# Retention and a multiplicative feed-forward on one core: loads put ahead of stores, scalings cut loose from the transposes, products moved to VectorE

## The chip, the core and the metric

The program runs on one of the eight cores of a Trainium2 chip. The metric is the device time of one execution in microseconds: 1075.24 us, the median of three runs (1071.42 to 1076.22). In the rows below, PE is TensorE's matmul, PEld its weight load, DVE VectorE, ACT ScalarE, POOL GpSimd and SP the engine whose queue issues nearly all DMAs.

## What is computed

A retention block (attention without a softmax, with a decay), and a feed-forward whose two branches are multiplied:

```
scores = q @ k.T / sqrt(64)                    # 8 batches x 8 heads, 576 positions, 64 wide
ret    = (scores * gamma_h ** (i - j), 0 for j > i) @ v
x      = ret, heads side by side               # 4608 tokens x 512
a, b   = x @ w1, x @ w2                        # 4608 x 1024 each
out    = ((a * b) @ w3) @ w_out                # 4608 x 512
```

The weights are given as 64-bit floats, the rest as 32-bit floats.

## The kernel before

**Attention.** Batches are taken in four pairs (i). A sequence of 576 is cut into five chunks of 64, 128, 128, 128 and 128 positions (c); g = 5 i + c counts the chunks. For each g, `load` brings k, q and v of the pair from memory (two buffers each). `front` scales q and v by the decay on GpSimd and transposes k and q on TensorE (`tp`), ScalarE copying the results. `state` multiplies k and v into a running state (`st`), which ScalarE copies to `sb`. `score` multiplies q and k, and VectorE masks the result (`pm`). `pv` adds the state's and the masked scores' share of the output (`xps`), which ScalarE copies to `xT`.

**Feed-forward.** The tokens of a pair are cut into three blocks of 2 x 192. `up(i, n, fp)` computes a quarter of a and b for one block by Strassen's scheme with seven products of half size, each of eight matmuls of 192 columns: the weight sums S1 to S4 are made once per quarter (`strassen_weights`), the token sums T once per block (`strassen_tokens`, on GpSimd). The seven products are put together by sums on VectorE (`plus`), and a times b goes to `ab`: one of the four slices on VectorE, three on GpSimd. w3 and w_out are multiplied with each other once (`w3_tr`, `w3_mm`), and `down` multiplies `ab` with the result, 128 tokens at a time, and stores it.

**Conversion.** The weights arrive as 40 blocks of 128 x 512 64-bit numbers in `raw` tiles and are made into 32-bit ones in five VectorE steps and two Relus on ScalarE each: three steps (`begin_block`: exponent e, mantissa m, low word added) and two (`end_block`: sign, product), with one block begun ahead of the one that is ended. The steps are a generator, and `convert(n)` draws n of them wherever it is called; this decides where they stand on VectorE's queue. The first 16 blocks are w1 and w2, four for each quarter, then 8 of w_out and 16 of w3.

**Order.** The order of every engine is that of the code: nothing is rearranged, and an engine that waits holds all that is behind it. The program has three stretches. In the first, the five chunks of pair 0 are worked off with the conversion and the first three `up`; then come the remaining nine `up` of pair 0 with w3 and w_out. In the second, `down` of pair 0 fills the chunks of pair 1. After that the `up` and `down` of each pair are spread by `work` over the chunks of the next. The lines that the change and the prediction's steps touch are `front`, `load_block`, `begin_block`, `up`, `down` and the loops at the end.

Of the kernel before, what the change touches and what calls it, by code (L numbers as in the profile page):

```python
# [32 lines left out]
def kernel(  # L33
# [72 lines left out]
    dq = ffn.tile([P, 3, 2, TB], F32, tag="c", name="dq").rearrange("p a b s -> p (a b s)")[:H, :S]  # L106
    nc.scalar.dma_start(dq, decay_q)
    for c in range(NC):
        for b in range(2):
# [21 lines left out]

    def strassen_weights(fp):
        def tt(out, in0, in1, op):
            nc.gpsimd.tensor_tensor(out=A(fp, out), in0=A(fp, in0), in1=A(fp, in1), op=op)  # L134

        tt("S1", "A21", "A22", ALU.add)
        tt("S2", "S1", "A11", ALU.subtract)
        tt("S3", "A11", "A21", ALU.subtract)
        tt("S4", "A12", "S2", ALU.subtract)
# [3 lines left out]
    def load(g, names):  # L143
# [3 lines left out]
        for nm in names:  # L147
# [2 lines left out]
                t[:sz], src[nm][2 * i:2 * i + 2, :, starts[c]:starts[c] + sz, :].rearrange("b h p d -> p (b h) d"))  # L150
            live[nm, g] = t

    def front(g):
        c = g % NC
        sz = sizes[c]
        kn, qn, vn = live["k", g], live["q", g], live["v", g]
        for t, gam in ((qn, gq), (vn, gk)):
            nc.gpsimd.tensor_tensor(  # L158
                out=t[:sz], in0=t[:sz],
                in1=gam[:sz, c].rearrange("p b h -> p (b h)").unsqueeze(2).to_broadcast([sz, 2 * H, D]),  # L160
                op=ALU.mult)
# [91 lines left out]
    def load_block():  # L253
        n = loaded[0]
        if n == len(blocks):
            return
        key, w = blocks[n]
        t = raw.tile([P, CV, 2], I32, tag="raw", name="raw", bufs=4)
        if key[0] == "w12":
            _, fp, _, r = key  # L260
            src = w[2 * r * P:2 * (r + 1) * P, fp * QC:(fp + 1) * QC, :]
            for half in range(2):
                for_rows = src.rearrange("(c a d) n t -> a d c n t", a=2, d=D)[half ^ r]
                nc.sync.dma_start(t[heads[half]].rearrange("p (c n) t -> p c n t", c=2), for_rows)
# [18 lines left out]
    def begin_block():  # L283
        n = begun[0]
        t = live["raw", n]
        lo, hi = t[:, :, 0], t[:, :, 1]
        e = raw.tile([P, CV], I32, tag="exp", name="e")
        m = raw.tile([P, CV], I32, tag="man", name="m")
        vec = nc.vector


        vec.tensor_scalar(out=e, in0=hi, scalar1=1, scalar2=21,  # L292
                          op0=ALU.logical_shift_left, op1=ALU.logical_shift_right)
        relu = mybir.ActivationFunctionType.Relu
        nc.scalar.activation(e, e, relu, bias=lim[:, 0:1], scale=-1.0)  # L295
        nc.scalar.activation(e, e, relu, bias=lim[:, 1:2], scale=-2.0 ** 23)
        yield

        vec.tensor_scalar(out=m, in0=hi, scalar1=0x000FFFFF, scalar2=0x00100000,  # L299
                          op0=ALU.bitwise_and, op1=ALU.bitwise_or)  # L300
        yield
        vec.scalar_tensor_tensor(m.bitcast(F32), in0=lo.bitcast(U32), scalar=2.0 ** -32, in1=m,  # L302
                                 op0=ALU.mult, op1=ALU.add)
        live["em", n] = e, m
        begun[0] += 1
        yield
# [83 lines left out]
    def up(i, n, fp, conv=0):  # L390
        m = every.index((i, n))
        convert_up_to(4 * (fp + 1))
        if ("B", i, n) not in live:
            strassen_tokens(i, n)
        if fp == 0:
            live["ab", i, n] = (ab3 if m == 2 else ffn).tile([P, 2 * KF, TB], F32, tag="ab", name="ab")
        ab = live["ab", i, n]
        f = 4 * fp
# [12 lines left out]
        def plus(name, ps, sb, out=None):  # L411
            out = ffn.tile([P, 2, TB], F32, tag=name, name=name, bufs=1) if out is None else out
            nc.vector.tensor_add(out, ps, sb)  # L413
            convert(conv)
            return out


        c = ffn.tile([P, 3, 2, TB], F32, tag="c", name="c")
        p1 = product(None, "A11", "B11")
        p1s = ffn.tile([P, 2, TB], F32, tag="p1s", name="p1s", bufs=1)  # L420
        nc.scalar.copy(p1s, p1)
        u2 = plus("u2", product(None, "S2", "T2"), p1s)
        u3 = plus("u3", product(None, "S3", "T3"), u2)
        p5 = product(None, "S1", "T1")
        plus("c22", p5, u3, out=c[:, 2])
        plus("c21", product(None, "A22", "-T4"), u3, out=c[:, 1])
        product(p1, "A12", "B21")
        c11 = ffn.tile([P, TB], F32, tag="c11", name="c11")
        nc.scalar.copy(c11, p1[:, 0, :])  # L429
        nc.vector.tensor_mul(ab[:, f, :], p1[:, 1, :], c11)  # L430
        product(p5, "S4", "B22")
        plus("c12", p5, u2, out=c[:, 0])
# [5 lines left out]
    def down(i, n, t):  # L438
# [9 lines left out]
        while a < (t + 1) * P:  # L448
            b = a // TB
            e = min((b + 1) * TB, (t + 1) * P)  # L450
            r = (2 * i + b) * S + n * TB + a - b * TB
            nc.sync.dma_start(out[r:r + e - a, :], ot[a - t * P:e - t * P])
            a = e


    load(0, "kqv")
    load(1, "kqv")
    for _ in range(4):
        load_block()
    front(0)  # L460
    state(0)
    score(0)
    for g in range(NC):
        if g + 2 < NC:
            load(g + 2, "kvq")
        if g + 1 < NC:
            front(g + 1)
        pv(g)
# [27 lines left out]
    w3_part.close()  # L496


    pools["ot"] = ctx.enter_context(tc.tile_pool(name="ot", bufs=2, reuse_waits="tile"))
# [4 lines left out]
    open_attention(ctx)  # L504
    todo = [(down, 0, n, t) for n in range(2) for t in range(NT)]

    def add_pair(i):
# [12 lines left out]
            fn, *args = todo.pop(0)  # L520
            fn(*args)

    load(NC, "kqv")
    load(NC + 1, "kqv")
    work(1)
    front(NC)
    state(NC)
    score(NC)
    for g in range(NC, G):
        c = g % NC  # L530
        n = -(-len(todo) // (NC - c))
        if g + 2 < G:
            load(g + 2, "kv")
        if g + 1 < G:
            front(g + 1)
        if g + 2 < G:
            load(g + 2, "q")
        work((n + 1) // 2)
        pv(g)
        if g + 1 < G:  # L540
            state(g + 1)
            score(g + 1)
        work(n // 2)
        if c == NC - 1:
            add_pair(g // NC)
# [44 lines left out]
```

## Time and profile before

| | |
|---|---|
| median of three runs | 1075.24 us |
| profiled execution | 1074.96 us |
| its span, first to last instruction | 1073.2 us |
| mean granted clock of TensorE | 0.936 |
| TensorE matmul busy | 942.3 us (88%) |
| VectorE busy | 322.8 us (30%) |
| GpSimd busy | 216.5 us (20%) |
| ScalarE busy | 196.2 us (18%) |
| DMA | 59.69 MB, 56 GB/s over the span |

The shares are means over stretches with different limits: the first 320 us hold the conversion of the weights and more than half of VectorE's work, and TensorE's clock is below its upper level in many slices there. Reading starts with the stretches apart, and in each with who waits for whom.

### The profile page before, as it was taken

What the parts mean: (1) busy time and instruction counts of PE and PEld (TensorE: products, weight loads), DVE (VectorE), ACT (ScalarE), POOL (GpSimd) and SP (SyncE); (2) the same over time, 40 slices, a digit from 0 to 9 for tenths busy, and PEclk for the clock granted to TensorE, in tenths of its full rate; (3) what the DMA queues carried; (4) which work ended last, traced back from release to release, by engine and by line L of the source; (5) the groups of instructions that cost most, each with busy time, mean ns of one, the idle gap of its engine ahead of it and who ended that gap; (6) DMA issues with size and microseconds to landing.
All of it is one profiled execution on the core that took longest, in us unless ns stands there. A gap on an engine that the chain in (4) does not pass through costs nothing.

```text
span 1073.2 us, 14017 instructions
## 1 busy us (share of the span) xinstructions
PE 942.3 (88%) x6085; PEld 743.6 (69%) x6085; DVE 322.8 (30%) x581; ACT 196.2 (18%) x373; POOL 216.5 (20%) x159
## 2 busy tenths in 40 slices
PE   4456568899999787779898998999989999999998
PEld 4356468787644554479668688598687795959694
DVE  2445778865500100023112222122122230303120
ACT  2313323332311221111111111111111201000000
POOL 3142332311000311132204103113032020302110
PEclk9767879889999888889999998999999999999999
DMA  9744323322003732233030230212402000000000
GB/s 170 145 89 99 79 79 99 99 97 79 20 1 66 151 70 59 49 70 60 0 89 1 50 65 5 60 30 45 104 1 50 21 1 30 1 20 11 20 10 30
DMA packets 126382, 59.69 MB, mean 56 GB/s; under 512 B 114536, under 2 KB 114536, under 8 KB 126320
## 3 DMA queue, kind: packets, MB, share of 16 engines
q1 hardware_dynamic: 124992, 58.73, 24.0%
q8 instruction: 48, 0.79, 0.3%
q10 hardware_dynamic: 1328, 0.06, 0.1%
q14 instruction: 14, 0.11, 0.0%
HBM read 49.34 MB, written 9.44 MB: 55 GB/s over the span
## 4 chain that ended last, share of the span: by engine, by line
PE 75%; DVE 8%; DMA 6%; POOL 4%; issue 3%; ACT 2%; SPq 1%; ACTq 0%; POOLq 0%; DVEq 0%
PE up L407 36%; PE po L442 23%; PE ps L365 5%; DMA ld_q<-in_q_dram 4%; PE xps L233 3%; PE tp L169 3%; PE sc L184 2%; POOL ld_q L158 2%; DVE m L302 2%; DVE e L313 1%; PE xps L226 1%; POOL wS L134 1%; SPq L149 1%; PE st L205 1%; DVE m L299 1%
## 5 line engine op out<-in xcount | busy, mean ns | idle before, releaser
L442 PE MATMUL po<-w3o,ab 128*128 128x512 f32 x576 | 259.4, 609 | 0.0
L407 PE MATMUL up<-xT,wA 128*128 128x192 f32 x1152 | 225.6, 341 | 18.7 <-DVE wA L322 15.1
L407 PEld LDWEIGHTS up<-xT,wA 128*128 128x128 f32 x1152 | 201.9, 200 | 24.5 <-DVE wA L322 16.3
L442 PEld LDWEIGHTS po<-w3o,ab 128*128 128x128 f32 x576 | 111.6, 196 | 134.6 <-issue 133.0
L436 POOL TENSOR_TENSOR ab<-c 128x576 f32<-128x576 f32 x48 | 69.9, 1455 | 549.6 <-DVE c L413 540.7
L407 PE MATMUL up<-T,wS 128*128 128x192 f32 x768 | 149.0, 339 | 23.6 <-POOL wS L134 14.7
L407 PEld LDWEIGHTS up<-T,wS 128*128 128x128 f32 x768 | 135.1, 200 | 25.3 <-POOL wS L134 15.6
L187 DVE TENSOR_TENSOR pm<-sc,mask 128x512 f32<-128x512 f32 (+1 forms) x80 | 45.6, 629 | 280.9 <-PE sc L184 280.8
L413 DVE TENSOR_TENSOR u<-up,p1s 128x384 f32<-128x384 f32 x48 | 26.8, 557 | 263.2 <-PE up L407 176.5
L413 DVE TENSOR_TENSOR c<-up,u 128x384 f32<-128x384 f32 x144 | 80.0, 556 | 77.1 <-PE up L407 76.4
L158 POOL TENSOR_TENSOR ld_q<-ld_q,gq 128x1024 f32<-128x1024 f32 (+1 forms) x20 | 38.4, 1918 | 214.1 <-DMA ld_q<-in_q_dram 214.1
L169 PE MATMUL tp<-ident,ld_q 128*128 128x128 f32 (+1 forms) x160 | 26.4, 324 | 59.1 <-POOL ld_q L158 59.1
L407 PE MATMUL up<-xT,wS 128*128 128x192 f32 x384 | 72.7, 334 | 5.1 <-DVE c L413 5.1
L407 PE MATMUL up<-T,wA 128*128 128x192 f32 x384 | 70.4, 326 | 1.0 <-ACT ot L445 1.0
L407 PEld LDWEIGHTS up<-xT,wS 128*128 128x128 f32 x384 | 65.1, 194 | 6.5 <-DVE c L413 6.5
L445 ACT COPY ot<-po 128x512 f32<-128x512 f32 x36 | 21.1, 586 | 260.8 <-PE po L442 230.7
L407 PEld LDWEIGHTS up<-T,wA 128*128 128x128 f32 x384 | 63.7, 190 | 1.3 <-ACT ot L445 1.3
L169 PEld LDWEIGHTS tp<-ident,ld_q 128*128 128x128 f32 (+1 forms) x160 | 21.5, 175 | 62.2 <-POOL ld_q L158 62.2
L365 PE MATMUL ps<-wo,w3T 128*128 128x512 f32 x128 | 56.7, 595 | 1.2 <-ACT w3T L359 1.2
L429 ACT COPY c<-up 128x192 f32<-128x192 f32 x48 | 15.1, 315 | 228.4 <-PE up L407 228.4
L295 ACT ACTIVATE e<-e,lim 128x512 int32<-128x512 int32 x40 | 28.9, 722 | 134.6 <-DVE e L292 134.6
L365 PEld LDWEIGHTS ps<-wo,w3T 128*128 128x128 f32 x128 | 23.9, 190 | 28.9 <-issue 26.8
(51 smaller groups left out, 711.8 us busy)
## 6 DMA issues: line engine op xcount, KB each, us to landing
ld_k<-in_k_dram SPq DMA_DIRECT2D x16, 512.0 KB, 5.9
ld_q<-in_q_dram SPq DMA_DIRECT2D x16, 512.0 KB, 7.1
ld_v<-in_v_dram SPq DMA_DIRECT2D x16, 512.0 KB, 4.6
raw<-in_moe_w_dram SPq DMA_DIRECT2D x32, 256.0 KB, 4.6
raw<-in_moe_w_dram SPq DMA_DIRECT2D x16, 512.0 KB, 3.4
out_dram<-ot SPq DMA_DIRECT2D x24, 256.0 KB, 2.4
raw<-in_moe_w_out_dram SPq DMA_DIRECT2D x8, 512.0 KB, 3.5
out_dram<-ot SPq DMA_DIRECT2D x24, 128.0 KB, 2.4
```

Source lines behind the costliest of these rows:

```text
L158: nc.gpsimd.tensor_tensor(out=t[:sz], in0=t[:sz], in1=gam[:sz, c].rearrange("p b h -> p (b h)").unsqueeze(2).to_broadcast([sz, 2 * H, D]), ...
L169: nc.tensor.transpose(tp[:, p, :sz], src[:sz, h:h + 2, :].rearrange("p a d -> p (a d)"), ident[:sz, :sz])
L184: nc.tensor.matmul(sc[j][:sz, p, :sz], kT[hs, b, p, :sz], qT[hs, b, p, :sz], start=True, stop=True)
L187: nc.vector.tensor_mul(pm[:sz, b, j, :, :sz], sc[j][:sz, :, :sz], mask[:sz, :sz].unsqueeze(1).to_broadcast([sz, NP, sz]))
L233: nc.tensor.matmul(banks[r][heads[half], b, n, :sz], vs[:sz, b * H + 2 * p + j, :], pm[:sz, b, j, p, :sz], start=(c == 0 and m == 0), stop ...
L295: nc.scalar.activation(e, e, relu, bias=lim[:, 0:1], scale=-1.0)
L302: vec.scalar_tensor_tensor(m.bitcast(F32), in0=lo.bitcast(U32), scalar=2.0 ** -32, in1=m, op0=ALU.mult, op1=ALU.add)
L365: nc.tensor.matmul(ps, live["w3T", ft][:, g, :], live["wo"][:, g, :], start=(g == 0), stop=(g == KF - 1))
L407: nc.tensor.matmul(ps[:, w, :], a[:, w, r, :], b[:, r, :], start=(new and w == r == 0), stop=(w == r == 1), skip_group_check=True)
L413: nc.vector.tensor_add(out, ps, sb)
L436: nc.gpsimd.tensor_tensor(out=ab[:, f + 1:f + 4, :], in0=c[:, :, 0, :], in1=c[:, :, 1, :], op=ALU.mult)
L442: nc.tensor.matmul(po, ab[:, f, t * P:(t + 1) * P], live["w3o"][:, f, :], start=(f == 0), stop=(f == KF - 1))
```

## The change

The loads of q and k stand ahead of v's and of the stores, with v's behind `pv`; the scalings of q and v are calls of their own (`scale`), placed apart from the transposes; the first loads of pair 1 stand ahead of three `down` blocks' stores, which are kept in a list (`later`), with a third `ot` tile. The weight sums and the product a times b go from GpSimd to VectorE, the product over all four slices at once, and the sums of `up` work in place in one tile `c` of four slices instead of in tiles of their own. The copy of a's first slice to SBUF takes both slices. One more `raw` tile is loaded ahead; the Relus are issued behind the third step; and the calls of `convert` are spread anew: one step at each sum and one at each product instead of two at each sum, and the steps ahead of `score` instead of behind it.

```diff
     def strassen_weights(fp):
         def tt(out, in0, in1, op):
-            nc.gpsimd.tensor_tensor(out=A(fp, out), in0=A(fp, in0), in1=A(fp, in1), op=op)
+            nc.vector.tensor_tensor(out=A(fp, out), in0=A(fp, in0), in1=A(fp, in1), op=op)
...
+    def scale(g, nm):
+        c = g % NC
+        sz = sizes[c]
+        t, gam = live[nm, g], {"q": gq, "v": gk}[nm]
+        nc.gpsimd.tensor_tensor(
+            out=t[:sz], in0=t[:sz],
+            in1=gam[:sz, c].rearrange("p b h -> p (b h)").unsqueeze(2).to_broadcast([sz, 2 * H, D]),
+            op=ALU.mult)
...
-        t = raw.tile([P, CV, 2], I32, tag="raw", name="raw", bufs=4)
+        t = raw.tile([P, CV, 2], I32, tag="raw", name="raw", bufs=5)
...
         vec.scalar_tensor_tensor(m.bitcast(F32), in0=lo.bitcast(U32), scalar=2.0 ** -32, in1=m,
                                  op0=ALU.mult, op1=ALU.add)
+        relu = mybir.ActivationFunctionType.Relu
+        nc.scalar.activation(e, e, relu, bias=lim[:, 0:1], scale=-1.0)
+        nc.scalar.activation(e, e, relu, bias=lim[:, 1:2], scale=-2.0 ** 23)
...
-        def plus(name, ps, sb, out=None):
-            out = ffn.tile([P, 2, TB], F32, tag=name, name=name, bufs=1) if out is None else out
-            nc.vector.tensor_add(out, ps, sb)
+        def plus(ps, to, sb):
+            nc.vector.tensor_add(c[:, to], ps, c[:, sb])
             convert(conv)
...
+        c = ffn.tile([P, 4, 2, TB], F32, tag="c", name="c")
         p1 = product(None, "A11", "B11")
-        p1s = ffn.tile([P, 2, TB], F32, tag="p1s", name="p1s", bufs=1)
-        nc.scalar.copy(p1s, p1)
-        u2 = plus("u2", product(None, "S2", "T2"), p1s)
...
+        nc.scalar.copy(c[:, 0], p1)
+        plus(product(None, "S2", "T2"), 1, 0)
+        plus(product(None, "S3", "T3"), 2, 1)
         p5 = product(None, "S1", "T1")
+        plus(p5, 3, 2)
+        plus(product(None, "A22", "-T4"), 2, 2)
         product(p1, "A12", "B21")
-        c11 = ffn.tile([P, TB], F32, tag="c11", name="c11")
-        nc.scalar.copy(c11, p1[:, 0, :])
-        nc.vector.tensor_mul(ab[:, f, :], p1[:, 1, :], c11)
+        nc.scalar.copy(c[:, 0], p1)
         product(p5, "S4", "B22")
+        plus(p5, 1, 1)
...
-        nc.gpsimd.tensor_tensor(out=ab[:, f + 1:f + 4, :], in0=c[:, :, 0, :], in1=c[:, :, 1, :], op=ALU.mult)
+        nc.vector.tensor_mul(ab[:, 4 * fp:4 * fp + 4, :], c[:, :, 0, :], c[:, :, 1, :])
+        convert(conv)
...
     for g in range(NC):
-        if g + 2 < NC:
-            load(g + 2, "kvq")
-        if g + 1 < NC:
-            front(g + 1)
+        if g + 1 < NC:
+            if g + 2 < NC:
+                load(g + 2, "kq")
+            scale(g + 1, "q")
+            front(g + 1)
+            scale(g + 1, "v")
         pv(g)
+        if g + 2 < NC:
+            load(g + 2, "v")
+        if g == 1:
+            strassen_tokens(0, 0)
         if g + 1 < NC:
             state(g + 1)
+            if g == 1:
+                convert_up_to(KD)
+            else:
+                convert(10)
             score(g + 1)
-        convert(10)
         if 0 < g < NC - 1:
             up(0, 0, g - 1, conv=1)
-            convert(6)
...
         if todo:
-            up(*todo.pop(0), conv=2)
+            up(*todo.pop(0), conv=1)
...
-        convert(10 if not todo else 2)
+        convert(10 if not todo else 3)
...
     for t in range(NT):
-        down(0, 2, t)
+        down(0, 2, t, later=True)
...
+    for g in (NC, NC + 1):
+        load(g, "kqv")
+    store()
...
     for g in range(NC, G):
         if g + 2 < G:
-            load(g + 2, "kv")
+            load(g + 2, "kq")
         if g + 1 < G:
+            scale(g + 1, "v")
             front(g + 1)
-        if g + 2 < G:
-            load(g + 2, "q")
         work((n + 1) // 2)
         pv(g)
+        if g + 2 < G:
+            load(g + 2, "v")
         if g + 1 < G:
             state(g + 1)
             score(g + 1)
+        if g + 2 < G:
+            scale(g + 2, "q")
         work(n // 2)
```

On SP's queue, in the second stretch, these rows stand behind one another in the kernel before: the stores of `down` (`out_dram`) and the loads of two chunks.

```order
L452 DMA out_dram<-ot 128x512
L149 DMA ld_k<-in_k_dram 128x16x64
L149 DMA ld_v<-in_v_dram 128x16x64
L149 DMA ld_q<-in_q_dram 128x16x64
L452 DMA out_dram<-ot 64x512 x2
L149 DMA ld_k<-in_k_dram 128x16x64
L149 DMA ld_v<-in_v_dram 128x16x64
L149 DMA ld_q<-in_q_dram 128x16x64
```

And these stand there now:

```order
L149 DMA ld_k<-in_k_dram 128x16x64
L149 DMA ld_q<-in_q_dram 128x16x64
L460 DMA out_dram<-ot 64x512 x2
L149 DMA ld_v<-in_v_dram 128x16x64
L149 DMA ld_k<-in_k_dram 128x16x64
L149 DMA ld_q<-in_q_dram 128x16x64
```

The load of q no longer stands behind that of the same chunk's v, but behind the v of the chunk before it; the store of the `down` in between stands ahead of v.

At the start of the second stretch the loads of pair 1 follow the stores of the first `down` blocks on SP in the kernel before:

```order
L267 DMA raw<-in_moe_w_dram 128x1024 x16
L452 DMA out_dram<-ot 128x512
L452 DMA out_dram<-ot 64x512 x2
L452 DMA out_dram<-ot 128x512
L149 DMA ld_k<-in_k_dram 64x16x64
L149 DMA ld_q<-in_q_dram 64x16x64
```

Now they follow the last load of weights:

```order
L271 DMA raw<-in_moe_w_dram 128x1024 x16
L149 DMA ld_k<-in_k_dram 64x16x64
L149 DMA ld_q<-in_q_dram 64x16x64
L149 DMA ld_v<-in_v_dram 64x16x64
L149 DMA ld_k<-in_k_dram 128x16x64
L149 DMA ld_q<-in_q_dram 128x16x64
L149 DMA ld_v<-in_v_dram 128x16x64
L460 DMA out_dram<-ot 128x512
```

All six loads moved past the stores.

On VectorE, between the first and the second `up` block, these rows stood in the kernel before (c is the sum of `up`, e, m and wA the conversion, pm the masked scores):

```order
L413 TENSOR_TENSOR c<-up,u_516 128x384
L322 SCALAR_TENSOR_TENSOR wA<-m,e 128x2x256
L292 TENSOR_SCALAR e<-raw 128x512
L299 TENSOR_SCALAR m<-raw 128x512
L302 SCALAR_TENSOR_TENSOR m<-raw,m 128x512
L313 SCALAR_TENSOR_TENSOR e<-raw,e 128x512
L322 SCALAR_TENSOR_TENSOR wA<-m,e 128x2x256
L292 TENSOR_SCALAR e<-raw 128x512
L187 TENSOR_TENSOR pm<-sc,mask 128x512 x4
```

Now the masks and the weight sums (wS) stand like this, with the product (ab) eleven conversion steps ahead of the masks, of which the last three are shown:

```order
L317 SCALAR_TENSOR_TENSOR e<-raw,e 128x512
L326 SCALAR_TENSOR_TENSOR wA<-m,e 128x2x256
L296 TENSOR_SCALAR e<-raw 128x512
L191 TENSOR_TENSOR pm<-sc,mask 128x512 x4
L300 TENSOR_SCALAR m<-raw 128x512
L303 SCALAR_TENSOR_TENSOR m<-raw,m 128x512
L317 SCALAR_TENSOR_TENSOR e<-raw,e 128x512
L326 SCALAR_TENSOR_TENSOR wA<-m,e 128x2x256
L134 TENSOR_TENSOR wS<-wA 128x512
L134 TENSOR_TENSOR wS<-wS,wA 128x512
```

Eleven steps now stand between the block and the masks, where six stood behind the block's last sum and its step; four are left behind the masks, where ten stood, and the weight sums follow them on the same queue.

On ScalarE, ahead of the first `up` block, the Relus (L295 and L296 before) stood like this:

```order
L295 ACTIVATE e<-e,lim 128x512
L296 ACTIVATE e<-e,lim 128x512
L172 COPY kT<-tp 128x512 x2
L172 COPY qT<-tp 128x512 x2
L237 COPY xT<-xps 128x2x2x128 x2
L209 COPY sb<-st 128x512
```

The same copies now, with the Relus of blocks 2 and 3 (L306 and L307) behind them:

```order
L176 COPY kT<-tp 128x512 x2
L176 COPY qT<-tp 128x512 x2
L241 COPY xT<-xps 128x2x2x128 x2
L213 COPY sb<-st 128x512
L306 ACTIVATE e<-e,lim 128x512
L307 ACTIVATE e<-e,lim 128x512
L306 ACTIVATE e<-e,lim 128x512
L307 ACTIVATE e<-e,lim 128x512
```

Before, three blocks' Relus stood ahead of those copies, now two.

## Rows read from the trace of the kernel before

**Rows 1.** Busy by stage: span, PE, PEld, DVE, ACT, POOL (counts), clock, DMA share, GB/s.

```profile
0.00:319.50 319.50, 239.59 (x1525) 198.06 (x1526) 175.58 (x305) 94.65 (x162) 74.59 (x57) 0.87 0.36 89
319.50:468.50 149.00, 115.88 (x898) 72.22 (x897) 12.84 (x24) 26.95 (x52) 26.54 (x15) 0.87 0.42 84
468.50:1073.20 604.70, 586.80 (x3664) 473.31 (x3663) 134.37 (x252) 74.62 (x159) 115.37 (x88) 0.99 0.14 31
```

**Rows 2.** TensorE's waits from 319.5 to 468.5: us in total, times, longest.

```profile
PE tp L169 <- POOL ld_q L158: 32.0, 6, 6.9
```

**Rows 3.** TensorE's waits from 468.5 to the end.

```profile
PE tp L169 <- POOL ld_q L158: 12.7, 4, 3.3
```

**Rows 4.** Chain of waits, second stage: start us, us, what.

```profile
366.32 6.84 DMA ld_q<-in_q_dram
...
387.02 1.92 PE xps L233 x32
389.00 0.37 SPq L149
```

**Rows 5.** TensorE's timeline, first stage: start, us, engine, line, operation.

```profile
64.27 2.93 PE L407 MATMUL up<-T,wS 128*128 128x192 f32 x8 [8.91 <-POOL T L381]
...
75.11 1.04 PE L169 MATMUL tp<-ident,ld_k 128*128 128x128 f32 x8
...
99.06 2.93 PE L407 MATMUL up<-T,wS 128*128 128x192 f32 x8 [4.86 <-POOL wS L134]
...
132.53 2.93 PE L407 MATMUL up<-T,wS 128*128 128x192 f32 x8 [4.92 <-POOL wS L134]
...
156.66 2.93 PE L407 MATMUL up<-T,wS 128*128 128x192 f32 x8 [4.92 <-POOL wS L134]
...
217.52 1.92 PE L357 MATMUL tp<-ident,w 128*128 128x128 f32 x8
```

**Rows 6.** VectorE's timeline, first stage.

```profile
77.93 2.12 DVE L299 TENSOR_SCALAR m<-raw 128x512 int32<-128x512 int32 x1
...
88.35 2.48 DVE L187 TENSOR_TENSOR pm<-sc,mask 128x512 f32<-128x512 f32 x4 [4.20 <-PE sc L184]
...
93.61 0.42 DVE L299 TENSOR_SCALAR m<-raw 128x512 int32<-128x512 int32 x1
...
95.39 0.69 DVE L322 SCALAR_TENSOR_TENSOR wA<-m,e 128x512 f32<-128x512 f32 x1
```

**Rows 7.** GpSimd's timeline, the same place.

```profile
77.69 2.08 POOL L158 TENSOR_TENSOR ld_q<-ld_q,gq 128x1024 f32<-128x1024 f32 x1
```

**Rows 8.** Chain of waits, last stage, work that follows on itself.

```profile
599.50 0.93 PE st L205 x32
...
616.35 1.75 PE tp L169 x16
618.10 6.87 PE po L442 x16
624.96 9.10 PE up L407 x56
634.06 1.03 PE xps L226 x32
635.10 1.90 PE xps L233 x32
637.00 1.99 PE sc L184 x32
```

**Rows 9.** Line 413: count, duration min/median/max in ns, first and last start.

```profile
L413 DVE TENSOR_TENSOR c<-up,u x144: 543/558/562, 71.4 to 1049.1; 128x384 f32<-128x384 f32 x144
```

**Rows 10.** ScalarE's timeline, first stage.

```profile
45.33 0.59 ACT L209 COPY sb<-st 128x512 f32<-128x512 f32 x1
```

**Rows 11.** The page's costliest groups: busy us, mean ns, idle before, releaser.

```profile
L295 ACT ACTIVATE e<-e,lim 128x512 int32<-128x512 int32 x40 | 28.9, 722 | 134.6 <-DVE e L292 134.6
```

**Rows 12.** GpSimd's groups over the span, same columns.

```profile
L381 POOL TENSOR_TENSOR T<-xT,T 128x384 f32<-128x384 f32 x24 | 24.6, 1025 | 12.5 <-PE up L407 11.7
```

More of the change, by code (lines that the diff above doesn't have):

```diff
@@ L105 @@
     gq = const.tile([P, NC, 2, H], F32, tag="gq", name="gq")
-    dq = ffn.tile([P, 3, 2, TB], F32, tag="c", name="dq").rearrange("p a b s -> p (a b s)")[:H, :S]
+    dq = ffn.tile([P, 4, 2, TB], F32, tag="c", name="dq").rearrange("p a b s -> p (a b s)")[:H, :S]
     nc.scalar.dma_start(dq, decay_q)
@@ L155, in front @@
         sz = sizes[c]
[L156 to L161, printed above, removed]
+        kn, qn = live["k", g], live["q", g]
         kT = pools["fr"].tile([P, 2, NP, P], F32, tag="kT", name="kT", bufs=1)
@@ L397, in up @@
         ab = live["ab", i, n]
-        f = 4 * fp
         def product(ps, a, b):
@@ L409, in product, with down @@
             return ps
-        def plus(name, ps, sb, out=None):
-            out = ffn.tile([P, 2, TB], F32, tag=name, name=name, bufs=1) if out is None else out
-            nc.vector.tensor_add(out, ps, sb)
+        def plus(ps, to, sb):
+            nc.vector.tensor_add(c[:, to], ps, c[:, sb])
             convert(conv)
-            return out
-        c = ffn.tile([P, 3, 2, TB], F32, tag="c", name="c")
+        c = ffn.tile([P, 4, 2, TB], F32, tag="c", name="c")
         p1 = product(None, "A11", "B11")
-        p1s = ffn.tile([P, 2, TB], F32, tag="p1s", name="p1s", bufs=1)
-        nc.scalar.copy(p1s, p1)
-        u2 = plus("u2", product(None, "S2", "T2"), p1s)
-        u3 = plus("u3", product(None, "S3", "T3"), u2)
+        nc.scalar.copy(c[:, 0], p1)
+        plus(product(None, "S2", "T2"), 1, 0)
+        plus(product(None, "S3", "T3"), 2, 1)
         p5 = product(None, "S1", "T1")
-        plus("c22", p5, u3, out=c[:, 2])
-        plus("c21", product(None, "A22", "-T4"), u3, out=c[:, 1])
+        plus(p5, 3, 2)
+        plus(product(None, "A22", "-T4"), 2, 2)
         product(p1, "A12", "B21")
-        c11 = ffn.tile([P, TB], F32, tag="c11", name="c11")
-        nc.scalar.copy(c11, p1[:, 0, :])
-        nc.vector.tensor_mul(ab[:, f, :], p1[:, 1, :], c11)
+        nc.scalar.copy(c[:, 0], p1)
         product(p5, "S4", "B22")
-        plus("c12", p5, u2, out=c[:, 0])
+        plus(p5, 1, 1)
         if fp == NQ - 1 and m + 1 < len(every) and has_x(*every[m + 1]):
             strassen_tokens(*every[m + 1])
-        nc.gpsimd.tensor_tensor(out=ab[:, f + 1:f + 4, :], in0=c[:, :, 0, :], in1=c[:, :, 1, :], op=ALU.mult)
-    def down(i, n, t):
+        nc.vector.tensor_mul(ab[:, 4 * fp:4 * fp + 4, :], c[:, :, 0, :], c[:, :, 1, :])
+        convert(conv)
+    def down(i, n, t, later=False):
         ab = live["ab", i, n].rearrange("p (f b) s -> p f (b s)", b=2)
@@ L451, in down, with store @@
             r = (2 * i + b) * S + n * TB + a - b * TB
-            nc.sync.dma_start(out[r:r + e - a, :], ot[a - t * P:e - t * P])
+            stores.append((out[r:r + e - a, :], ot[a - t * P:e - t * P]))
             a = e
+        if not later:
+            store()
+    stores = []
+    def store():
+        while stores:
+            nc.sync.dma_start(*stores.pop(0))
     load(0, "kqv")
     load(1, "kqv")
-    for _ in range(4):
+    for _ in range(5):
         load_block()
+    scale(0, "q")
     front(0)
+    scale(0, "v")
     state(0)
@@ L463 @@
     for g in range(NC):
+        if g + 1 < NC:
[4 more added lines that the diff above has]
+            scale(g + 1, "v")
+        pv(g)
         if g + 2 < NC:
-            load(g + 2, "kvq")
-        if g + 1 < NC:
-            front(g + 1)
-        pv(g)
+            load(g + 2, "v")
+        if g == 1:
+            strassen_tokens(0, 0)
         if g + 1 < NC:
             state(g + 1)
+            if g == 1:
+                convert_up_to(KD)
+            else:
+                convert(10)
             score(g + 1)
-        convert(10)
         if 0 < g < NC - 1:
             up(0, 0, g - 1, conv=1)
-            convert(6)
     att_part.close()
@@ L494 @@
             turned[0] += 1
-        convert(10 if not todo else 2)
+        convert(10 if not todo else 3)
     w3_part.close()
-    pools["ot"] = ctx.enter_context(tc.tile_pool(name="ot", bufs=2, reuse_waits="tile"))
+    pools["ot"] = ctx.enter_context(tc.tile_pool(name="ot", bufs=3, reuse_waits="tile"))
     for t in range(NT):
-        down(0, 2, t)
+        down(0, 2, t, later=True)
     weights_part.close()
@@ L504 @@
     open_attention(ctx)
+    for g in (NC, NC + 1):
+        load(g, "kqv")
+    store()
     todo = [(down, 0, n, t) for n in range(2) for t in range(NT)]
@@ L521, in work @@
             fn(*args)
-    load(NC, "kqv")
-    load(NC + 1, "kqv")
+    scale(NC, "q")
+    scale(NC, "v")
     work(1)
@@ L528 @@
     score(NC)
+    scale(NC + 1, "q")
     for g in range(NC, G):
```

3 lines of the change are left out of this document (removed).

## The prediction

> **What bounds the kernel now.** I read the busy time by stage first, then TensorE's waits, then the chain of waits inside each stage, then the timelines of single engines. The stages differ [rows 1]: up to 319.5 us TensorE is busy 239.6 of 319.5 us at a granted clock of 0.87; from there to 468.5 us 115.9 of 149.0, again 0.87; behind that 586.8 of 604.7 at 0.99. So the last stage is TensorE's own time and has little to give; the first two hold the idle time, and their busy time is stretched besides, because the clock falls to its lower level after idling.
>
> In the second stage one wait stands out: the transposes of q, held for 32.0 us in six places by the scaling on POOL, and 12.7 us in four more in the last stage [rows 2, 3]. The chain shows what lies behind it [rows 4]: when the attention product of one chunk ends (388.9), SP issues ld_v, then ld_q; like the one before it (issued at 366.3, 6.84 us), that ld_q takes some 6 to 7 us to land, POOL scales for about 2 [rows 7], and only then do the transposes run. The cause is SP's order: ld_v may not be issued before `pv` has read the old v, and ld_q stands behind it.
>
> In the first stage the S2·T2 products of the first four `up` blocks start at 64.27, 99.06, 132.53 and 156.66, each time after 4.9 to 8.9 us without work, ended by POOL [rows 5]. They wait for POOL's four weight sums (the first for T behind these), and these for VectorE's conversion. VectorE itself is slowed: a step that takes 0.42 us takes 2.12 while POOL scales for 2.08 [rows 6, 7].
>
> **Part by part.** The sum is against the profiled 1074.96 us (span 1073.2 and 1.8 around it), which is 0.3 below the median of 1075.24.
>
> *Loads, second stage.* k and q of chunk g+2 now stand ahead of v, at the head of the iteration; their old tiles are free by then. v still waits for `pv`, but its scaling is wanted only by `state`, one iteration later. Per iteration TensorE works 1.75 + 6.87 + 2.93 + 0.93 + 1.99 = 14.5 us [rows 8]. From the end of `pv(g-1)`, v, k and q land one behind another: a single landing is 6.84 [rows 4], and two more loads of 0.5 MB add some 2.5 each (an estimate from 84 GB/s at a DMA share of 0.42 [rows 1], so 200 GB/s at full share): q is there after 12 and scaled after 14; its transposes come 17 us after. So all six waits are hidden, by 3 us. If that cover is gone, each is worth only what it falls short. The first six loads of the next pair move ahead of the stores of `down(0, 2, t)`, to when the conversion frees the raw tiles, some 20 us before the stage; four `down` blocks (27 us) follow on TensorE. The stores queue behind the loads, which is what the third `ot` tile covers.
> What then remains of 149.0 us is work: nine `down` (61.8), seven transposes at 1.75 (12.3), five `pv` at 2.93 (14.7), five `state` (4.7), six `score` (11.9), 105 less about 4 since the 64-row chunks cost half: 101 [rows 8]. I add 3 for small waits: 104, **saves 45** (bounds: 20 if the loads still come late by half, 48 if nothing waits).
>
> *Loads, last stage.* The four waits (12.7) go by the same order; a clock of 0.99 over 604.7 us is 6 us more, of which I take 4 back: **saves 17** (8 to 20).
>
> *First stage, the first four blocks.* Weight sums (4 per block, 16) and the product go to VectorE. No such operation with both inputs in SBUF and this opcode is in the trace. Nearest: a sum of 384 columns from PSUM 0.558, a two-input step of 512 columns 0.69 [rows 6, 9]; so 0.69 for a weight sum and, by that slope, 0.95 for the product of 768 columns. Lower bound 0.56 for either (the sum of 384); upper bound 0.69 or 0.95 plus one POOL operation of 2.08. I take the undisturbed values and add locks where POOL works beside.
> First S2·T2: block 4 no longer has to wait for a raw tile (five of them), so conversion is held by ScalarE, where the two Relus of block 2 now stand behind the copy of `sb` (45.33 + 0.59 [rows 10]). They end at 47.4 (0.72 each [rows 11]); then eight steps at 0.57 (2.9 us for five [rows 6]), without overlap of the last, and S1, S2 of 0.61 behind one another: 53.1. POOL's T operations (1.03 each [rows 12]) and a scaling lie beside: + 2.4. S2·T2 starts at 55.5 instead of 64.3.
> Each block then runs 10.8 us (64.27 to 75.11 [rows 5]). From its end to the next S2·T2: product 0.95, eight steps 4.6, but the Relus wait behind `front`, `pv`, `state` and the `sb` copy: 2.0 + 3.1 + 0.95 (TensorE not at full clock) + 0.59 + 1.44 = 8.1 us; then three steps 1.7, the masks 2.5 [rows 6], four steps 2.4, S1 and S2 1.3: 16.0, and 1.6 of lock. Spacing 28.4 (before 34.8). The next has no `state` and no lock: 26.3 (33.5). The fourth has no masks: 0.95 + 15 steps 8.6 + 1.3 + 10.8 = 21.7 (24.1). The fourth start falls at 131.9 instead of 156.66: **saves 24.8** (bounds 8 and 35).
>
> *The next five blocks*, to 217.52 [rows 5], took 60.9 us. VectorE had 12 steps a block there; now 9: 5.1, five sums 2.8, product 0.95, 8.9 against 9.10 on TensorE [rows 8]. With 9.3 a block, and 10.7 for the first: 48, **saves 12.9** (5 to 15). The cover is thin: one more us of lock each makes 2.4 us in all.
>
> *From 217.52 to 319.5* TensorE is busy nearly throughout; **saves 2** (-3 to 4): the rest of the conversion (8 of 40 blocks behind the last `up`, 23 us) fits beside 46 us of weight products.
>
> *Behind that* the product on VectorE costs nothing I can see: five sums and it make 3.7 of 9.1 us a block; it ends about 1.5 us after the block, and `down` reads its last columns 5 us later. The scalings apart from the transposes, the wider `c11` copy on ScalarE and the in-place sums: nothing, for the same slack.
>
> Sum: 24.8 + 12.9 + 2 + 45 + 17 = 101.7; 1074.96 - 101.7 = **973 us**.
>
> [...]
>
> **Rivals.**
> 1. *The conversion stays held in the first stage.* The Relus behind the `sb` copy, and the masks between the steps, keep the spacing where it is; only POOL's sums go (3 x 2.5) and a part of the later gain. Savings there fall from 39.7 to about 8: 1005. For it: VectorE and ScalarE run in order, and three blocks a stage still wait for `state`. Against: VectorE's idle 4 to 10 us a stage now hold steps.
> 2. *Loads still late.* v waits for `pv`, and k and q of the next chunk stand behind it on SP; if landing takes 12 us instead of 7, ten waits of about 4 us stay: 973 + 40 = 1013. Against: the DMA share is 0.42 there.
> 3. *More is won*: the conversion runs wholly beside TensorE, and the first four blocks gain 35, the others 15, the loads 68: 1074.96 - 122 = 953, down to 948 with the smaller waits gone.
> 4. *Slower.* The place is VectorE's queue between one block's product and the next block's first sum. If TensorE had to wait there for the product and a POOL operation that blocks it, every one of 48 blocks would lose 0.95 + 1.9 = 2.85: 137 us, so 1110. It decides from the point where VectorE's work per block passes 9.1 us: in the five middle blocks it is at 8.9, behind 319.5 us at 3.7, so 36 of the 48 have 5 us of slack. [...]
>
> **Numbers.** Forecast 0.74, rival 1 0.11, rival 2 0.06, rival 3 0.06, rival 4 0.03. Range: the terms' bounds together would reach 948 to 1037, but they do not all fall the same way; 948 to 1008 takes in rivals 1 and 3 and leaves out rival 2, rival 4 and the forecast's own tail, about 0.18. Half a per cent (5.4 us) is about what a measurement of this kernel can tell from no change. Faster 0.96, same 0.01, slower 0.03.
>
> **What would show it.** Right: no wait of the transposes for POOL after the first stage, and six loads issued before the first store; the second pair's first `up` about 45 us earlier relative to the end of the weight products; S2·T2 starts near 55, 84, 110 and 132 ended by VectorE, not POOL; middle blocks at 9.1 to 9.5 us; the clock of the second stage near 1.0. Wrong: S2·T2 still ending waits of 5 us at a spacing over 30; ld_q landing after its scaling is due; TensorE waiting on the product in the last stage.

## The result and the profile after

The changed kernel takes 973.84 us (median of four runs, 973.25 to 976.48) against 1075.38 before: a ratio of 0.9067, 95% interval 0.9039 to 0.9095. The forecast was 973.0, range 948 to 1008. The profiled execution took 976.48 us (span 974.7), so the trace accounts for 98.5 us, between 1074.96 and 976.48.

Busy time by stage of the changed kernel, to be held against [rows 1] (span, PE, PEld, DVE, ACT, POOL with counts, clock, DMA share, GB/s); the stages are cut at the first `down` and at the start of pair 1's first `up`, which is at 468.27 in the kernel before, 0.2 us ahead of the cut there:

```profile
0.00:283.20 283.20, 228.43 (x1525) 188.73 (x1526) 180.16 (x321) 96.66 (x162) 41.61 (x33) 0.91 0.47 108
283.20:384.54 101.34, 101.34 (x898) 63.26 (x896) 12.75 (x24) 25.31 (x52) 17.11 (x9) 1.00 0.46 94
384.54:974.70 590.16, 581.27 (x3666) 470.63 (x3664) 156.39 (x252) 80.49 (x161) 67.25 (x53) 0.99 0.15 33
```

The stages shrink by 36.3, 47.7 and 14.5 us. In the second, TensorE is busy throughout; its busy time fell from 115.9 to 101.3 us for the same work, because the granted clock rose from 0.87 to 1.00.

TensorE's waits in the first stage, the largest rows (us in total, times, longest):

```profile
PE up L410 <- DVE wS L134: 21.2, 4, 6.8
PE tp L173 <- DMA ld_k<-in_k_dram: 11.6, 2, 9.7
PE up L410 <- DVE wA L326: 7.3, 4, 3.9
PE tp L173 <- POOL ld_q L157: 5.0, 2, 2.6
```

and from 283 us to the end, where this is the only one, in place of the ten waits of 44.7 us for the scaled q [rows 2, 3]:

```profile
PE up L410 <- POOL T L385: 5.4, 1, 5.4
```

TensorE's timeline in the first stage, the rows that answer to [rows 5]:

```profile
57.24 2.90 PE L410 MATMUL up<-T,wS 128*128 128x192 f32 x8 [6.76 <-DVE wS L134]
...
83.92 2.90 PE L410 MATMUL up<-T,wS 128*128 128x192 f32 x8 [5.86 <-DVE wS L134]
...
110.25 2.90 PE L410 MATMUL up<-T,wS 128*128 128x192 f32 x8 [5.87 <-DVE wS L134]
...
132.23 2.90 PE L410 MATMUL up<-T,wS 128*128 128x192 f32 x8 [2.75 <-DVE wS L134]
...
180.29 1.46 PE L410 MATMUL up<-xT,wA 128*128 128x192 f32 x8
```

The waits are little shorter (21.2 us in all, where they were 23.6), but VectorE ends them, and the products behind them start 7.0, 15.1, 22.3 and 24.4 us earlier. The row at 180.29 begins the block after the five middle ones; before, those ended at 217.52.

The chain of waits in the second stage, which answers to [rows 4] (start us, us, what):

```profile
322.76 1.08 PE xps L237 x32
323.84 1.08 PE st L209 x32
324.93 1.99 PE sc L188 x32
326.91 1.90 PE tp L173 x16
328.81 6.87 PE po L441 x16
...
380.87 6.38 DMA ld_v<-in_v_dram
...
389.27 1.00 POOL T L385
```

Transposes, `down`, `pv`, `state` and `score` follow one another with nothing between. At the end of the stage the chain leaves TensorE for the wait for T named above. GpSimd's timeline there (start, us; in brackets the idle time before and what ended it):

```profile
387.41 1.90 POOL L157 TENSOR_TENSOR ld_v<-ld_v,gk 128x1024 f32<-128x1024 f32 x1 [7.37 <-DMA ld_v<-in_v_dram]
389.27 0.99 POOL L385 TENSOR_TENSOR T<-xT 128x384 f32<-128x384 f32 x1
```

The token sums T need nothing that is still on its way: they stand on GpSimd's queue behind the scaling of v, and that waits for a load issued behind `pv`.

VectorE's groups by line, over the span (busy us, mean ns, idle time before and its releaser):

```profile
L415 DVE TENSOR_TENSOR c<-up,c 128x384 f32<-128x384 f32 x240 | 133.6, 557 | 373.4 <-PE up L410 371.2 <-ACT c L421 1.1
L434 DVE TENSOR_TENSOR ab<-c 128x768 f32<-128x768 f32 x48 | 46.2, 962 | 3.8
...
L134 DVE TENSOR_TENSOR wS<-wA 128x512 f32<-128x512 f32 x4 | 2.8, 692 | 0.1
```

### The profile page after: what moved, and what is told of

It is laid out like the page before. It is cut to its first block, busy times and chain, and to the rows that moved or that the text cites. A ratio compares the mean times of both kernels' runs of the same rounds, so it can differ in the third digit from the quotient of the medians.

```text
span 974.7 us, 14094 instructions
## 1 busy us (share of the span) xinstructions
PE 911.0 (93%) x6085; PEld 722.6 (74%) x6085; DVE 349.3 (36%) x597; ACT 202.5 (21%) x373; POOL 126.0 (13%) x95
## 4 chain that ended last, share of the span: by engine, by line
PE 87%; DVE 6%; DMA 3%; ACT 1%; SPq 1%; issue 1%; POOL 0%; ACTq 0%; POOLq 0%; DVEq 0%
PE up L410 45%; PE po L441 25%; PE ps L369 5%; PE xps L237 3%; PE tp L173 3%; PE sc L188 3%; PE xps L230 2%; PE st L209 1%; DMA ld_q<-in_q_dram 1%; DVE e L317 1%; DVE m L303 1%; DVE wA L326 1%; DMA raw<-in_moe_w_dram 1%; DMA ld_v<-in_v_dram 1%; SPq L149 1%
## 5 line engine op out<-in xcount | busy, mean ns | idle before, releaser
L415 DVE TENSOR_TENSOR c<-up,c 128x384 f32<-128x384 f32 x240 | 133.6, 557 | 373.4 <-PE up L410 371.2
L441 PE MATMUL po<-w3o,ab 128*128 128x512 f32 x576 | 251.0, 593 | 0.0
L410 PE MATMUL up<-xT,wA 128*128 128x192 f32 x1152 | 219.4, 334 | 7.3 <-DVE wA L326 7.3
L410 PEld LDWEIGHTS up<-xT,wA 128*128 128x128 f32 x1152 | 196.5, 195 | 12.7 <-DVE wA L326 8.5
L441 PEld LDWEIGHTS po<-w3o,ab 128*128 128x128 f32 x576 | 108.2, 190 | 129.2 <-issue 128.4
L410 PE MATMUL up<-T,wS 128*128 128x192 f32 x768 | 148.8, 339 | 26.6 <-DVE wS L134 21.2
L428 ACT COPY c<-up 128x384 f32<-128x384 f32 x48 | 23.0, 479 | 259.3 <-PE up L410 259.2
L385 POOL TENSOR_TENSOR T<-xT,T 128x384 f32<-128x384 f32 x24 | 24.6, 1025 | 346.9 <-PE up L410 346.7
L157 POOL TENSOR_TENSOR ld_v<-ld_v,gk 128x1024 f32<-128x1024 f32 (+1 forms) x20 | 38.3, 1915 | 169.6 <-DMA ld_v<-in_v_dram 162.9
L434 DVE TENSOR_TENSOR ab<-c 128x768 f32<-128x768 f32 x48 | 46.2, 962 | 3.8
L306 ACT ACTIVATE e<-e,lim 128x512 int32<-128x512 int32 x40 | 28.9, 723 | 66.3 <-DVE e L296 66.2
L188 PE MATMUL sc<-qT,kT 64*128 64x128 f32 (+1 forms) x640 | 38.6, 271 | 0.0
```

The costliest lines, as they stand in the source:

```text
L157: nc.gpsimd.tensor_tensor(out=t[:sz], in0=t[:sz], in1=gam[:sz, c].rearrange("p b h -> p (b h)").unsqueeze(2).to_broadcast([sz, 2 * H, D]), ...
L188: nc.tensor.matmul(sc[j][:sz, p, :sz], kT[hs, b, p, :sz], qT[hs, b, p, :sz], start=True, stop=True)
L385: nc.gpsimd.tensor_tensor(out=out, in0=in0, in1=in1, op=ALU.subtract)
L415: nc.vector.tensor_add(c[:, to], ps, c[:, sb])
L434: nc.vector.tensor_mul(ab[:, 4 * fp:4 * fp + 4, :], c[:, :, 0, :], c[:, :, 1, :])
L441: nc.tensor.matmul(po, ab[:, f, t * P:(t + 1) * P], live["w3o"][:, f, :], start=(f == 0), stop=(f == KF - 1))
```

## The experiments

The kernels are cut from before (the first) or from the changed one, and each is compared with before on the same chip: the first four on one chip (before 1072.11 there), the others on a second (1073.89), so that a difference between kernels of the two groups, or to the changed kernel, carries some 2 to 3 us, as the times of before do (1075.38, 1072.11 and 1073.89). Diffs show the edit against the kernel named.

**1. The loads alone**, put into the kernel before: is the second stage theirs, and the last one's four waits too?

```diff
     for g in range(NC, G):
         if g + 2 < G:
-            load(g + 2, "kv")
+            load(g + 2, "kq")
         if g + 1 < G:
             front(g + 1)
-        if g + 2 < G:
-            load(g + 2, "q")
         work((n + 1) // 2)
         pv(g)
+        if g + 2 < G:
+            load(g + 2, "v")
```

with the first six loads of pair 1 ahead of the stores of two `down` blocks (two `ot` tiles allow no more).

> The kernel before with the loads' order of the pairs alone: k and q of chunk g+2 at the head of the iteration, v behind pv, and the six first loads of pair 1 ahead of two of the three first stores (two ot tiles leave room for no more). Scalings stay inside front, sums of weights and product on GpSimd, conversion as before. Theory, as the two traces now read: the second stretch falls from 149.0 us to about 105, since its waits are for landing; the four waits of the last stretch (12.7 us) stay, since there the scaling of q stands behind the product ab on GpSimd and not behind a load: 1075.4 - 44 = 1031 us. Rival A, as the prediction had it: the order of the loads removes those four waits too: 1014 us. Rival B: without the scalings apart, the loads alone hide little: over 1055 us.

Measured: 1030.61 us, 0.9617 (0.9597 to 0.9637). TensorE's waits from 319 us on:

```profile
PE tp L169 <- POOL ld_q L158: 12.7, 4, 3.3
PE up L407 <- POOL T L381: 4.7, 1, 4.7
```

The second stage takes 101.4 us at a clock of 1.00, without a wait. The four waits of the last stage stay to the tenth of a microsecond: they are not the loads'. The wait for T is there already, so it comes with the new order of the loads.

**2. The loads undone** in the changed kernel (the diff above backwards, and no `later` stores).

> The changed kernel with the loads of the pairs as before (k and v at the head, q behind front, the first three downs' stores ahead of the six loads); all else as changed. Theory: the second stretch gets its landing waits back, 973.8 + 45 = 1019 us, and the last stretch has no wait of the transposes for GpSimd, since the product is off it. Rival A: the four waits of the last stretch come back too: 1035 us. Rival B: the scalings apart hide half of the landing: 996 us.

Measured: 1014.64, 0.9465 (0.944 to 0.9489). Busy by stage, the second and the last:

```profile
281.80:426.55 144.75, 112.38 (x897) 70.15 (x896) 12.83 (x24) 26.84 (x52) 26.30 (x14) 0.88 0.43 86
426.55:1009.90 583.35, 579.75 (x3665) 469.57 (x3664) 157.72 (x252) 79.98 (x159) 65.30 (x53) 1.00 0.14 32
```

The second stage is nearly the old one again (144.8 us of 149.0, with seven waits for the scaled q, 31.2 us), and the last has no wait at all: 583.4 us against 604.7 before and 590.2 in the changed kernel. So the rest of the change takes 21.3 us out of the last stage, and the new order of the loads puts 6.8 back.

**3. Weight sums and product back on GpSimd**, all else as changed.

```diff
-            nc.vector.tensor_tensor(out=A(fp, out), in0=A(fp, in0), in1=A(fp, in1), op=op)
+            nc.gpsimd.tensor_tensor(out=A(fp, out), in0=A(fp, in0), in1=A(fp, in1), op=op)
...
-        nc.vector.tensor_mul(ab[:, 4 * fp:4 * fp + 4, :], c[:, :, 0, :], c[:, :, 1, :])
+        nc.gpsimd.tensor_tensor(out=ab[:, 4 * fp:4 * fp + 4, :], in0=c[:, :, 0, :], in1=c[:, :, 1, :], op=ALU.mult)
```

> The changed kernel with the sums of weights and the whole product ab (four slices, so 768 columns, some 1.9 us by the slope of GpSimd's groups of 384 and 576) back on GpSimd. Theory: each of the first four S2 products starts 1.2 us later for the slower sums, and three of them up to 1.9 us more for one product that blocks VectorE: the fourth at 142 instead of 132 us; the next blocks lose about 0.5 us each; the last stretch nothing, since the scaling of q now stands ahead of the blocks' products: 973.8 + 12 = 986 us. Rival A: the transposes wait for GpSimd again in the last stretch: 999 us. Rival B: GpSimd's work was the whole of the first stretch's gain of 36 us: 1010 us.

Measured: 993.66, 0.9272 (0.925 to 0.9293), between the theory's 986 and rival A's 999; rival A's cause is absent, since no transposes wait in the last stage. The first four blocks start 34.5, 33.6 and 24.3 us apart, as before the change. The chain of waits between the first two shows what the theory left out:

```profile
65.98 0.04 POOL ab L434
...
66.11 1.95 issue
68.06 2.09 POOL ld_q L157
...
70.19 1.97 PE tp L173 x8
72.16 1.92 PE xps L230 x32
74.08 3.08 PE xps L237 x32
77.16 0.96 PE st L209 x32
...
78.14 0.58 ACT sb L213
78.72 0.63 ACT e L306
...
79.38 0.73 ACT e L307
...
80.13 0.70 DVE e L317
```

The product is first on GpSimd's queue, then the scaling of q; behind it come the transposes, `pv` and `state` on TensorE, the copy of the state on ScalarE, the Relus behind that copy, and at last the conversion. Here the product on GpSimd costs mainly by this detour, and not by its own time.

**4. The conversion as it was** (drawn behind `score`, two steps a sum, none behind the product), all else as changed.

```diff
             state(g + 1)
-            if g == 1:
-                convert_up_to(KD)
-            else:
-                convert(10)
             score(g + 1)
+        convert(10)
         if 0 < g < NC - 1:
             up(0, 0, g - 1, conv=1)
+            convert(6)
```

> The changed kernel with the conversion's steps called where they were: ten behind score instead of ahead of it, six behind the up block, two at each sum instead of one, none at the product, two instead of three at the loop's end. Sums and product stay on VectorE, loads as changed. Theory: three times 4 us of VectorE idle before the masks come back, and VectorE's work per block in the middle rises to 6.8 + 2.8 + 0.95 = 10.6 us against 9.1 on TensorE for five blocks, 7 us: 973.8 + 18 = 992 us. Rival A: the spread is worth nothing once GpSimd no longer blocks VectorE: 974 us. Rival B: it is the whole of the first stretch's gain: 1010 us.

Measured: 981.55, 0.9155 (0.913 to 0.918): 7.7 us of the change, where the theory had 18. The fourth S2·T2 starts at 138.22 instead of 132.23, and the waits for the conversion (`wA`) grow from 7.3 to 19.6 us while those for the sums shrink from 21.2 to 13.5. Of the 6.0 us at the fourth start 4.4 are there at the first already (61.68 instead of 57.24), and the next five blocks take 50.9 instead of 48.1 us, where the theory had put 7 more. The places of the steps and their numbers were changed together, so what each is worth stays open.

**5. The product alone on GpSimd** (the second half of experiment 3's diff): does it explain that experiment by itself?

> The changed kernel with the product ab alone back on GpSimd (768 columns, 1.87 us there), the sums of weights on VectorE. Theory, from the run with both back (993.7 us): the product stands ahead of the scaling of q on GpSimd in the first stretch, so the transposes behind an up block wait some 4 us, and with them state, the copy of sb, the Relus and the conversion; of the 20 us lost there this is the larger part, 4 to 5 us at each of three spacings: 973.8 + 14 = 988 us, S2 spacings near 32, 31 and 23 us. Rival: the slower sums of weights were the larger part (2.5 us at each of four starts and more): 979 us.

Measured: 990.88, 0.9235 (0.9209 to 0.9262). The first four blocks start 32.2, 31.4 and 23.7 us apart, as expected. By the medians the product's move is worth 17.0 us. In the two traces it is 14.0, all in the first stage: the first `down` begins at 297.2 instead of 283.2, and what follows takes 690.3 instead of 691.5. The detour lengthens the first two spacings by 5.5 and 5.1 us; the third, which has no transposes, grows by 1.7. Against that the first S2·T2 starts 2.4 us earlier, at 54.83: two scalings stand behind the first block's product here, and no longer beside two steps of the conversion (the last two rows of VectorE's timeline under experiment 8), which take 0.43 and 0.42 us here instead of 2.01 and 2.12. The weight sums have some 3 left (993.66 to 990.88; 5.5 between the traces). In the last stage no transposes wait here either.

**6. The scalings together again**, at the head of `front` with q first, all else as changed (the product on VectorE).

```diff
         if g + 1 < G:
+            scale(g + 1, "q")
             scale(g + 1, "v")
             front(g + 1)
...
-        if g + 2 < G:
-            scale(g + 2, "q")
         work(n // 2)
```

and the same in the loop over pair 0; the scaling of q ahead of this loop goes as well.

> The changed kernel with both scalings at the head of front again, q first (sums and product on VectorE, loads as changed). Theory: the four waits of the last stretch came from GpSimd's queue, and with the product off it only the sums of tokens T can stand ahead of the scaling of q: waits of up to 4 us at one to three chunks, so 973.8 to 984 us, 977 as one number; the second stretch stays near 104 us. Rival A: the product's move alone removes the four waits, and the scalings apart are worth nothing: 974 us. Rival B: the scalings apart are what removes them: 990 us.

Measured: 973.19, 0.9069 (0.9047 to 0.909), the changed kernel's time; rival A was right. Its only wait from 285 us on:

```profile
PE up L410 <- POOL T L385: 4.3, 1, 4.3
```

With the product off GpSimd, the scaling of q is early enough at either place. By experiment 5 the reverse holds as well: with the scalings apart, the product on GpSimd does not delay the transposes of the last stage. Either half removes the four waits.

**7. The new wait removed**: in the one iteration where the tokens meet it, v is scaled behind them.

```diff
         if g + 1 < G:
-            scale(g + 1, "v")
+            if g != 2 * NC:
+                scale(g + 1, "v")
             front(g + 1)
         work((n + 1) // 2)
+        if g == 2 * NC:
+            scale(g + 1, "v")
```

> The changed kernel with one call moved: in the iteration in which pair 1 has its first up block, the scaling of v is issued behind the work, so that the sums of tokens T no longer stand behind a scaling that waits for its load. Theory: TensorE's wait of 5.4 us for T goes, and about 1.5 us of a block at the lower clock with it: 973.8 - 6 = 968 us. Rival: v's scaling is then late for state, and the same time is lost there: 974 us.

Measured: 966.25, 0.9005 (0.8983 to 0.9026), 7.6 us below the changed kernel. The wait was 5.4; the clock explains a part of the rest. The stretch with the wait and the one behind it, in the changed kernel, and then the last stage of this one:

```profile
387.00:395.00 8.00, 3.61 (x11) 3.61 (x12) 0.56 (x1) 0.00 (x0) 7.51 (x6) 0.72 0.40 82
395.00:410.00 15.00, 15.00 (x87) 15.00 (x87) 5.43 (x9) 0.96 (x2) 1.05 (x2) 0.92 0.00 1
```

```profile
382.74:964.40 581.66, 578.10 (x3666) 467.76 (x3664) 156.51 (x252) 80.50 (x161) 63.42 (x49) 1.00 0.15 33
```

At 0.92, 15.0 busy us are 1.2 more than at 1.00, and the 3.6 busy us before them ran lower still. Now the clock is 1.00 over the whole stage, which takes 581.7 us instead of 590.2.

**8. The conversion ahead of the state**, on top of experiment 7. In the changed kernel VectorE idles until the Relus end, which stand on ScalarE behind the copy of the state. VectorE's timeline there:

```profile
46.99 1.11 DVE L317 SCALAR_TENSOR_TENSOR e<-raw,e 128x512 int32<-128x512 int32 x1 [12.97 <-ACT e L307]
48.14 1.37 DVE L326 SCALAR_TENSOR_TENSOR wA<-m,e 128x512 f32<-128x512 f32 x1
49.54 2.01 DVE L296 TENSOR_SCALAR e<-raw 128x512 int32<-128x512 int32 x1
51.47 2.12 DVE L300 TENSOR_SCALAR m<-raw 128x512 int32<-128x512 int32 x1
```

```diff
     for g in range(NC):
+        if g == 1:
+            convert_up_to(KD)
         if g + 1 < NC:
...
-            state(g + 1)
-            if g == 1:
-                convert_up_to(KD)
-            else:
+            if g != 1:
                 convert(10)
+            state(g + 1)
             score(g + 1)
```

> As the run before, and in the first stretch the conversion is called ahead of state: for the second chunk already at the head of its iteration, so that the Relus no longer stand behind the copy of sb, for which VectorE sat idle for 13 us until 47 us. Theory: the first S2 product starts near 48 us instead of 57, when T is there, the next ones 1 us closer: 968 - 10 = 958 us, S2 starts near 48, 74, 99, 121. Rival A: raw blocks land too late for this, or pass the loads of the third chunk's q, which is then late: 968 us. Rival B: VectorE is the bound of the three stages behind it, and takes half of it back: 963 us.

Measured: 956.03, 0.891 (0.8887 to 0.8932): 10.2 us below experiment 7 and 17.8 below the changed kernel, the best of all. TensorE's timeline, the same four products as above:

```profile
49.11 1.46 PE L410 MATMUL up<-T,wS 128*128 128x192 f32 x8
...
73.33 2.90 PE L410 MATMUL up<-T,wS 128*128 128x192 f32 x8 [5.87 <-DVE wS L134]
...
99.03 2.90 PE L410 MATMUL up<-T,wS 128*128 128x192 f32 x8 [5.87 <-DVE wS L134]
...
120.68 2.90 PE L410 MATMUL up<-T,wS 128*128 128x192 f32 x8 [2.75 <-DVE wS L134]
```

The first wait is gone, and the fourth start is 11.6 us earlier. Two waits of 5.87 stay; moving the masks, which stand 2.5 us long among the steps, was not tried.

## Why the prediction was right

Each term, as predicted and as the profiled executions have it:

| term | predicted | measured | from |
|---|---|---|---|
| first four blocks | 24.8 | 24.4 | 156.66 to 132.23 |
| next five blocks | 12.9 | 12.8 | 60.86 to 48.06 |
| rest of the first stage | 2 | -0.9 | 101.98 to 102.91 |
| second stage | 45 | 47.7 | 149.0 to 101.3 |
| last stage | 17 | 14.5 | 604.7 to 590.2 |
| sum | 101.7 | 98.5 | 1074.96 to 976.48 |

**First stage: right in size, the cause of the old loss named only in part.** The starts forecast at 55.5, 84, 110 and 132 came at 57.24, 83.92, 110.25 and 132.23. That the fourth fits so well is partly luck: the first start came 1.7 us late, since the seven steps between the Relus and the first weight sum took 8.7 us (46.99 to 55.68) where eight steps and their lock (the prediction's word for what GpSimd adds to a step) were put at 7.0, and the first spacing came 1.7 short, 26.7 instead of 28.4, since the lock of 1.6 put there did not come. The weight sum was taken at 0.69 us and measures 0.692, the product at 0.95 and measures 0.962. Experiments 3 to 5 share the stage out: with the product on GpSimd the first `down` comes 14.0 us later, with the weight sums there as well another 5.5, with the old spread 6.5 (17.0, 2.8 and 7.7 by the medians); runs whose first stage is the changed kernel's differ there by up to 1.8 (281.4 to 283.2). The prediction blamed mainly the sums for the old waits, since the profile names them as the last to arrive [rows 5] (from the second block on two of the four, as in its sum: S2·T2 at 99.06 follows the second, which ends at 99.00); the product, which no row of TensorE's waits named as such, weighs more than twice as much. In the kernel before it stands on GpSimd's queue just ahead of the scaling of [rows 7], for which the transposes behind the block wait:

```profile
75.95 1.78 POOL L436 TENSOR_TENSOR ab<-c 128x576 f32<-128x576 f32 x1 [9.83 <-DVE c L413]
```

```profile
79.82 1.35 PE L169 MATMUL tp<-ident,ld_q 128*128 128x128 f32 x8 [3.67 <-POOL ld_q L158]
```

The prediction's spacings have no such wait in them, which is right for the changed kernel, but it did not say that the product's move is what takes it away. The parts add up to some 26 to 28 of the stage's 36.3; the other 8 to 10 (the fifth `raw` tile, the sums in place, and what the parts do together) were not taken apart.

**Second stage: right in cause, a little short in size.** Experiments 1 and 2 do and undo the loads: -41.5 from before (1072.11 in that comparison) and +40.8 from the changed kernel. Of the stage's 47.7 us idle time has 33.1 (the six waits 32.0) and the clock the rest: busy time fell by 14.5 us with the same work. The work was put at 101 us and took 101.3; the 3 added for small waits did not come. The cover was there too: of three loads issued behind a `pv`, from 338.68 on, q was scaled from 348.88 to 350.78 and transposed at 357.00, so 6 us later, where the prediction had 3.

**Last stage: the size near, the step wrong.** "The four waits (12.7) go by the same order" of loads was the step that failed. Experiment 1 has that order, and the four waits are still there. GpSimd's timeline of the kernel before, at one of them, shows the reason:

```profile
519.89 1.40 POOL L436 TENSOR_TENSOR ab<-c 128x576 f32<-128x576 f32 x1 [7.70 <-DVE c L413]
521.24 1.90 POOL L158 TENSOR_TENSOR ld_q<-ld_q,gq 128x1024 f32<-128x1024 f32 x1
```

The scaling starts the moment the product ends, and the product had waited for `up`: q had long landed (its load was issued at 498.2 and took 6.4 us). "POOL ld_q" ended the wait in both stages, but a DMA was behind it in the one and a place in a queue in the other. The size came out near, 14.5 for 17, because two errors nearly cancelled, which is luck: the rest of the change, of which by experiments 5 and 6 the product's move or the scalings' alone removes the four waits, was worth 21.3 us, not 17 (in experiment 2 the stage's busy time fell by 7.1, from 586.8 to 579.8, where the prediction took 4 for the clock), and a wait that the prediction did not have, that for T, took 6.8 back. The step "its scaling is wanted only by `state`, one iteration later" overlooked who stands behind that scaling on GpSimd.

**The two engines' contention.** The step of 2.12 us in [rows 6] reads one tile, and so do those of lines 296 and 300 above: they take 2.01 and 2.12 us beside GpSimd's scalings, and 0.43 and 0.42 in experiment 5, where no scaling lies beside them. So a step need not have two inputs in SBUF to be held up. The Trainium skill, "SBUF — State Buffer", section "Who interferes with whom", says that a VectorE instruction with at most one SBUF input does not contend with GpSimd outside VectorE's two-port modes, and that steps of this kind can enter those. The trace agrees that such a step is held up; no row names its mode. In the sum this is the lock at the first start, put at 2.4 us: the four rows from 46.99 on take 6.6 us, where 0.69, 0.69, 0.43 and 0.42 are theirs undisturbed, so it was some 4.4.

**The rivals.** The conversion is still what the first four blocks wait for, but closer together than rival 1 had it. From the second stage on no load was late but the one of v whose scaling stands ahead of T; in the first, TensorE waits 11.6 us for k (9.0 before), which no rival had. TensorE's wait for the product, rival 4, appears nowhere; of the five blocks' 48.06 us the first has 10.7, as assumed, which leaves 9.3 for each other, beside the 8.9 us of VectorE's work. The bounds of the terms add up to 953 to 1037 us; the 948 said of them is rival 3's with the smaller waits gone.

## What to carry to other kernels

Where a profile says that an engine waits for an operation, ask before crediting a cure what that operation itself waited for: one timeline row tells a late transfer from an engine that was busy with something else, and the cures differ. An operation off the critical path on an in-order engine costs what it holds up behind it, through every queue on the way; the products of 1.9 us on GpSimd cost 14 to 17 us in the first stage. And a load that is moved behind something moves with it all that its consumer's queue holds, here the token sums behind the scaling of v.

## What the runs showed of the hardware

Where VectorE and GpSimd collided, both took longer. VectorE and GpSimd in experiment 8:

```profile
39.10 0.69 DVE L326 SCALAR_TENSOR_TENSOR wA<-m,e 128x512 f32<-128x512 f32 x1
39.83 2.27 DVE L134 TENSOR_TENSOR wS<-wA 128x512 f32<-128x512 f32 x1
```

```profile
39.35 2.20 POOL L157 TENSOR_TENSOR ld_v<-ld_v,gk 128x1024 f32<-128x1024 f32 x1 [1.44 <-DMA ld_v<-in_v_dram]
```

GpSimd's 1.90 becomes 2.20: 39.35 to 39.79 lie under VectorE's instruction. Then VectorE's 0.69 becomes 2.27, ending 0.55 after GpSimd's (41.55 to 42.10). A product of 768 columns takes 962 ns on VectorE; on GpSimd it is 1874 (mean of 48 in experiment 3). And a wait of 5.4 us cost 7.6 by the medians and 8.5 in the last stage of the traces: the granted clock was 0.72 over the 8 us around its end and 0.92 over the next 15, and 1.00 in the same stage without the wait.
